# A second product whose two column groups are both 64 columns wide, in a recurrence with capacity-limited experts behind it

## The chip, the cores and the metric

The kernel runs on one core of one Trainium2 chip. The metric is the device time of one execution in microseconds (us). All inputs start in device memory (HBM) and the output ends there.

## The reference

Two blocks follow each other. The first is a gated recurrence over 4 sequences of 5,056 steps with 256 channels. The second takes its 20,224 rows as tokens, chooses one of 8 experts for each, keeps the 80 tokens of each expert with the highest gate, and gives only these an output; all other rows are zero.

```python
for t in range(S):
    h = f[:, t] * h + i[:, t] * x[:, t]
    y[:, t] = h
...
for e in range(E):
    ...
        keep = np.argpartition(-gw, capacity)[:capacity]
        tok_idx = tok_idx[keep]
    h = np.maximum(x[tok_idx] @ w1[e], 0.0)
    out[tok_idx] = gate_w[tok_idx, None] * (h @ w2[e])
```

`w1[e]` is 256 x 1024, `w2[e]` is 1024 x 256, both float32, so each is 1 MB. `h @ w2[e]` is the second product.

## The kernel before

The work goes through three stretches. In the first (to about 115 us) f and x are streamed in, turned with TensorE, scanned on VectorE and kept on chip as `h_all`; the router's logits are made on the way. In the second the 80 best tokens of each expert are ranked (lines 377 to 700) and their column numbers land in `trow`. In the third, the function `experts` (line 708), the tokens are collected, sent through the two products and scattered to the output. The change lies in the third alone.

`experts` runs over the 8 experts, e = 0 to 7. `gather(e)` (lines 717 to 728) copies 80 single columns of `h_all` into a tile `xe`; three engines share them, 24 on DVE, 32 on ACT and 24 on POOL, and each loads its column numbers from `trow` into registers first (line 723). `scaled(e)` (line 731, POOL) multiplies `xe`. `hidden(e)` (line 747, PE) is the first product: 32 matmuls, two for each of 2 x 8 pairs of a half of `w1` and a chunk of 128 hidden units. The two matmuls of a pair load 64 stationary columns each and write PSUM partitions 0 to 63 and 64 to 127, which are two column groups of the array; 80 columns move through. `relu(e)` brings the hidden values into the tile `hid`, the first half on ACT (line 754) and the second on DVE (line 755). `result(e)` (line 763, PE) is the second product: 8 chunks `c`, and for each chunk two matmuls with the hidden values of 64 and of 16 tokens as stationary columns, through which the 256 columns of a chunk of `w2` move into `y_ps`. `finish(e)` (line 771, DVE) multiplies by the gate into a row tile, and `scatter(e)` (line 775, POOL) is an indirect DMA of 80 rows to the output.

The order of the work is written out by hand in lines 799 to 839; nothing reorders it. Before the loop stand `gather` and `scaled` for experts 0, 1 and 2, `hidden(0)`, and two groups of idle matmuls (`busy`, line 160). Then, for each e: `relu(e)`, `hidden(e+1)`, `gather(e+3)`, `scaled(e+3)`, `result(e)`, `finish(e)`. So PE runs hidden(1), result(0), hidden(2), result(1), ..., hidden(7), result(6), result(7). Scatters 0 and 1 are issued around `gather(7)`; scatters 2 to 7 come after the loop, and five of them are held back until a named matmul of `result` has run (`apart`, line 814). Scatter 7 waits until all others have landed. Scatter 0 waits until the output has been cleared.

The weights come as 32 halves of 512 KB on SP's queue, which also carries the copies that clear the output (`copied`, line 137). The halves go round in 7 slots (`half`, lines 509 to 520), so half k is issued when PE has used half k - 7. The halves stand in the order in which PE uses them; the copies stand between them at fixed places (`BETWEEN`).

Each float32 matmul shows as two records in the trace; the word record means this below.

Of the kernel before, what the change touches and what calls it, by code (L numbers as in the profile page):

```python
# [9 lines left out]
F32 = mybir.dt.float32  # L10
# [5 lines left out]
ACT = mybir.ActivationFunctionType  # L16
PSUM = bass.MemoryType.PSUM
P = 128
# [8 lines left out]
def kernel(  # L27
# [11 lines left out]
    nc = tc.nc  # L39
    B, S, D = x.shape  # L40
    E, _, F = w1.shape
    N = B * S
    DC = D // P
    FC = F // P
    R = 4
# [4 lines left out]
    K = (capacity + TOP - 1) // TOP * TOP  # L50
# [20 lines left out]
    FH, CH = F // 2, FC // 2  # L71
# [13 lines left out]
    def slot(i, name):  # L85
        return ring[i].tile([P, R * D], F32, name=name, tag="buf")
# [36 lines left out]
    gates = consts.tile([K, E], F32, name="gates")  # L123
# [7 lines left out]
    def copied():  # L131

        at = written[0]
        n = min(P * ZH, TOTAL - at)
        if n:
            z = 2 * ZH if n % (2 * ZH) == 0 else D
            nc.sync.dma_start(out=out_flat[ds(at, n)].rearrange("(p k) -> p k", k=z),
                              in_=out_flat[:n].rearrange("(p k) -> p k", k=z))
            written[0] += n
# [22 lines left out]
    with tc.tile_pool(name="gsm", bufs=1) as gsm:  # L162
# [239 lines left out]
        with tc.tile_pool(name="plg", bufs=1, space=PSUM) as plg, \  # L402
# [48 lines left out]
            with tc.tile_pool(name="pct", bufs=4, space=PSUM) as pct:  # L451
                cts = {}

                def turn(*runs):
                    ct = pct.tile([P, 4 * P], F32, name="ct", tag="ct")
                    for g0, g1 in runs:
                        turned(ct[:, ds((g0 - runs[0][0]) * P, (g1 - g0) * P)], g0, g1)
                        cts[g0] = ct, runs[0][0]
                    return ct
# [24 lines left out]
                c = turn((6, LAST - 1), (LAST - 1, LAST))  # L484
# [222 lines left out]

    def experts(again):
        with tc.tile_pool(name="xp", bufs=3) as xp, \
             tc.tile_pool(name="mp", bufs=2) as mp, \  # L710
             tc.tile_pool(name="rp", bufs=E - R) as rp, \
             tc.tile_pool(name="psh", bufs=4, space=PSUM) as psh, \
             tc.tile_pool(name="psy", bufs=2, space=PSUM) as psy:
            w = {} if again else w_sb
            late = list(halves_of if again else halves_of[NSLOT - 1:])
            X, HID, Y, rows = {}, {}, {}, {}
            sent, marks = [], {}

            def gather(e):
                X[e] = xp.tile([P, DC, K], F32, name="xe", tag="xe")  # L720
                k = 0
                for engine, copy, n in ways:
                    _, at_tok = nc.values_load_multi_w_load_instructions(
                        trow[ds(e, 1), ds(k, n)], engines=(engine,), min_val=0, max_val=N - 1,
                        skip_runtime_bounds_check_because="column numbers come from iota")
                    for j, v in enumerate(at_tok):
                        copy(X[e][:, :, ds(k + j, 1)], h_all[:, :, ds(v, 1)])  # L727
                    k += n

            def scaled(e):  # L730
                nc.gpsimd.tensor_tensor(X[e], X[e], omlb.unsqueeze(2).broadcast_to([P, DC, K]),  # L731
                                        ALU.mult)

            H = P // 2

            def hidden(e):
                HID[e] = mp.tile([P, FC, K], F32, name="hid", tag="hid")
                xt = X.pop(e)
                wo = [w.pop((1, e, o)) for o in range(DC)]
                ps = [psh.tile([P, CH, K], F32, name="h_ps", tag="h_ps") for _ in range(2)]  # L740
                for o in range(DC):
                    for k in range(2 * CH):
                        i, c = divmod(k, CH)
                        a, j = divmod(c, J)
                        for s in range(2):
                            at = i * FH + a * J * P + j + J * s * H
                            nc.tensor.matmul(  # L747
                                ps[i][ds(s * H, H), c], wo[o][:, at:at + J * (H - 1) + 1:J],
                                xt[:, o], start=o == 0 and c == 0, stop=o == DC - 1,
                                skip_group_check=True)  # L750
                return ps

            def relu(e, ps):
                nc.scalar.activation(HID[e][:, :CH], ps[0], ACT.Relu)  # L754
                nc.vector.tensor_scalar_max(HID[e][:, CH:], ps[1], 0.0)

            def result(e):
                halves = [w.pop((2, e, i)) for i in range(2)]
                hid = HID.pop(e)
                y = Y[e] = psy.tile([K, D], F32, name="y_ps", tag="y_ps")  # L760
                for c in range(FC):
                    for s0, n in ((0, H), (H, K - H)):
                        marks[e, c] = nc.tensor.matmul(  # L763
                            y[ds(s0, n)], hid[:, c, ds(s0, n)], halves[c // CH][:, c % CH],
                            start=c == 0, stop=c == FC - 1, skip_group_check=True)

            def finish(e):
                if e == 0:
                    rows["y"] = slot(0, "y").rearrange("p (t d) -> p t d", t=R)
                rows[e] = rows["y"][:K, e] if e < R else rp.tile([K, D], F32, name="y4", tag="y4")  # L770
                nc.vector.tensor_scalar_mul(rows[e], Y.pop(e), gates[:, ds(e, 1)])  # L771

            def scatter(e, behind=None):

                sent.append(nc.gpsimd.indirect_dma_start(  # L775
                    out=out, out_offset=bass.IndirectOffsetOnAxis(ap=goal[:, ds(e, 1)], axis=0),
                    in_=rows.pop(e), in_offset=None, bounds_check=N - 1, oob_is_err=False))
                if behind:
                    tc.add_manual_dep(sent[-1].ins, marks[behind].ins.name, mybir.DependencyInfo(
                        mybir.DependencyClass.Sync, mybir.DependencyReason.DATA), reason="apart")  # L780
                for other in sent[:-1]:
                    if e < E - 1:
                        tc.declare_no_dep(sent[-1].ins, other.ins, reason="other rows")
                    else:
                        tc.add_manual_dep(sent[-1].ins, other.ins.name, mybir.DependencyInfo(
                            mybir.DependencyClass.Sync, mybir.DependencyReason.DATA),
                            reason="all rows")

            def more(m):
                for _ in range(2 * m):  # L790
                    if late:
                        k = len(halves_of) - len(late)
                        key = late.pop(0)
                        w[key] = half(*key)
                        if not again:
                            for _ in range(BETWEEN.count(k)):
                                copied()

            if again:
                more(3)  # L800
            gather(0)
            scaled(0)
            if not again:
                busy(psy, 4, "y_ps")
            gather(1)
            scaled(1)
            gather(2)
            scaled(2)
            ps = hidden(0)
            more(1)  # L810
            if not again:
                busy(psy, 3, "y_ps")

            apart = {2: (E - 3, FC - 1), 3: (E - 2, 0), 4: (E - 2, FC - 1), 5: (E - 1, 1),
                     6: (E - 1, FC - 2)}
            for e in range(E):
                relu(e, ps)
                if e == 0 and not again:
                    gates_of(slots[:, 1])
                if e + 1 < E:  # L820
                    ps = hidden(e + 1)
                    more(1)
                if e == E - 4:
                    scatter(0)
                if e + 3 < E:
                    gather(e + 3)
                    scaled(e + 3)
                if e == E - 4:
                    scatter(1)
                result(e)  # L830
                more(1)
                finish(e)
                if e == 0 and not again:
                    found = consts.tile([1, 1], F32, name="found")
                    nc.vector.tensor_reduce(found, total, AX.X, ALU.add)
                    nc.vector.tensor_copy(doubt, found)
                    rows_of(consts, slots[:, 0], slots[:, 1])
            for e in range(2, E):
                scatter(e, apart.get(e))
# [6 lines left out]
    with tc.If(unsure > 0):  # L846
        with tc.tile_pool(name="all", bufs=1) as sel, \
# [37 lines left out]
            rp = psa.tile([E, K], F32, name="rp")  # L885
# [46 lines left out]
```

## Time and profile before

| | us |
|---|---|
| median of 3 runs (252.64 to 252.92) | 252.69 |
| the profiled execution, its own time | 253.41 |
| its span in the trace | 251.5 |

| engine | busy us | share of the span |
|---|---|---|
| PE | 221.4 | 88% |
| DVE | 156.8 | 62% |
| ACT | 133.1 | 53% |
| POOL | 143.2 | 57% |

The busy shares are averages over three stretches that have different limits. For this change the third stretch, from about 142 us to the end, is the one to read: in order of time, and engine by engine. The span is 1.9 us shorter than the execution's own time; the rest lies around the traced instructions.

### The profile page before, as it was taken

To read this page: it belongs to the slowest core of one execution; us is meant where nothing else is said; L and a number is where in the kernel's file an instruction comes from. 1 tells how busy PE (TensorE), PEld (TensorE's weight loads), DVE (VectorE), ACT (ScalarE), POOL (GpSimd) and SP (SyncE) were. 2 spreads that over 40 slices of the span, in tenths; PEclk is the share of its full clock that TensorE was granted. 3 is DMA by queue.
4 is the path that set the end of the run, shared out by engine and by line. 5 is a ranking of instruction groups with operands and counts; after the bars stand their busy time and mean duration, and the time that the engine had idled before them with its cause. 6 is when DMAs were issued, how large, how long until landed. Compare 5 with 4: busy or idle time off the path is not lost.

```text
span 251.5 us, 6853 instructions
## 1 busy us (share of the span) xinstructions
PE 221.4 (88%) x2223; PEld 141.9 (56%) x2223; DVE 156.8 (62%) x400; ACT 133.1 (53%) x419; POOL 143.2 (57%) x287
## 2 busy tenths in 40 slices
PE   0699899899989998999966899799999999999960
PEld 0698787778868787777834646252525344352210
DVE  4189699999999999899999567435415051010100
ACT  4488798779787886888826066755042300000000
POOL 4678797889788798779844067650450620011211
PEclk9999999999999999999997979999999999999996
DMA  6999999999999999999999999969985474620000
GB/s 248 377 410 449 371 425 412 418 420 401 412 405 408 397 434 391 395 403 412 400 363 417 416 444 402 417 257 345 340 300 199 154 250 137 219 95 14 26 20 17
DMA packets 21363, 80.61 MB, mean 320 GB/s; under 512 B 2580, under 2 KB 2710, under 8 KB 20888
## 3 DMA queue, kind: packets, MB, share of 16 engines
q1 hardware_dynamic: 20936, 79.45, 80.4%
q0 software_dynamic: 384, 0.66, 0.9%
q8 instruction: 19, 0.31, 0.5%
q14 instruction: 24, 0.20, 0.2%
HBM read 72.62 MB, written 21.36 MB: 374 GB/s over the span
## 4 chain that ended last, share of the span: by engine, by line
PE 45%; issue 19%; ACT 10%; DVE 9%; DMA 9%; POOL 4%; ACTq 1%; DVEq 0%; POOLq 0%; SPq 0%
PE y_ps L763 14%; PE sp L251 11%; PE up L259 9%; PE lg L289 6%; DMA x_t<-in_x_dram 5%; ACT h_all L268 4%; ACT xe L727 3%; PE h_ps L747 3%; DMA f_t<-in_f_logit_dram 3%; DVE h_all L276 3%; POOL out_dram L775 2%; PE lt L313 2%; POOL x_t L245 2%; ACT ls L298 2%; DMA out_dram<-y,goal 1%
## 5 line engine op out<-in xcount | busy, mean ns | idle before, releaser
L245 POOL TENSOR_TENSOR x_t<-f_t,x_t 128x1024 f32<-128x1024 f32 x40 | 94.7, 2370 | 21.1 <-DMA x_t<-in_x_dram 10.6
L276 DVE TENSOR_TENSOR_SCAN h_all<-h_all,up 128x512 f32<-128x512 f32 (+1 forms) x80 | 95.8, 1244 | 9.9 <-PE up L259 6.4
L763 PE MATMUL y_ps<-w_sb,hid 128*64 128x256 f32 (+1 forms) x256 | 71.3, 393 | 1.4 <-ACT hid L754 1.4
L268 ACT ACTIVATE h_all<-sp,nomlb 128x512 f32<-128x512 f32 (+1 forms) x80 | 50.3, 677 | 16.5 <-PE sp L251 15.7
L763 PEld LDWEIGHTS y_ps<-w_sb,hid 128*64 128x64 f32 (+1 forms) x256 | 19.4, 115 | 50.4 <-issue 48.8
L241 ACT ACTIVATE f_t<-f_t 128x1024 f32<-128x1024 f32 x40 | 42.3, 1058 | 9.8 <-DMA f_t<-in_f_logit_dram 7.3
L259 PE MATMUL up<-ident,x_t 128*128 128x128 f32 x320 | 44.0, 278 | 2.8 <-DVE h_all L276 2.2
L251 PE MATMUL sp<-ident,f_t 128*128 128x128 f32 x320 | 45.4, 287 | 0.0
L251 PEld LDWEIGHTS sp<-ident,f_t 128*128 128x128 f32 x320 | 35.9, 145 | 7.8 <-issue 7.1
L259 PEld LDWEIGHTS up<-ident,x_t 128*128 128x128 f32 x320 | 36.7, 143 | 5.1 <-DVE h_all L276 3.7
L771 DVE TENSOR_SCALAR y<-y_ps,gates 80x256 f32<-80x256 f32 x8 | 3.8, 480 | 57.0 <-PE y_ps L763 51.5
L727 ACT COPY xe<-h_all 128x2 f32 x256 | 25.4, 190 | 18.8 <-issue 12.2
L727 POOL COPY xe<-h_all 128x2 f32 x192 | 24.3, 189 | 14.2 <-issue 7.0
L727 DVE COPY xe<-h_all 128x2 f32 x192 | 22.7, 173 | 12.0 <-issue 7.4
L775 POOL DMA_INDIRECT out_dram<-y,goal x8 | 7.5, 942 | 35.3 <-PE y_ps L763 31.1
L289 PE MATMUL lg<-h_all,wg 128*32 128x128 f32 (+1 forms) x640 | 26.4, 282 | 0.6 <-ACT ls L298 0.6
L754 ACT ACTIVATE hid<-h_ps 128x320 f32<-128x320 f32 x8 | 3.5, 435 | 39.2 <-PE h_ps L747 21.3
L747 PEld LDWEIGHTS h_ps<-xe,w_sb 128*64 128x64 f32 x512 | 18.2, 138 | 4.1 <-issue 3.6
L747 PE MATMUL h_ps<-xe,w_sb 128*64 128x80 f32 x512 | 19.5, 234 | 0.0
L289 PEld LDWEIGHTS lg<-h_all,wg 128*32 128x32 f32 x640 | 15.4, 108 | 7.0 <-issue 4.9
L731 POOL TENSOR_TENSOR xe<-xe,omlb 128x160 f32<-128x160 f32 x8 | 3.6, 452 | 23.5 <-DVE xe L727 22.1
L160 PE MATMUL warm<-h_all,ident 128*128 128x512 f32 x22 | 13.1, 740 | 0.0
(128 smaller groups left out, 105.6 us busy)
## 6 DMA issues: line engine op xcount, KB each, us to landing
f_t<-in_f_logit_dram SPq DMA_DIRECT2D x40, 512.0 KB, 6.6
x_t<-in_x_dram SPq DMA_DIRECT2D x40, 512.0 KB, 6.9
w_sb<-in_moe_w_dram SPq DMA_DIRECT2D x31, 512.0 KB, 5.0
out_dram<-out_dram SPq DMA_DIRECT2D x26, 512.0 KB, 8.2
out_dram<-zbuf SPq DMA_DIRECT2D x12, 512.0 KB, 10.0
out_dram<-h_all SPq DMA_DIRECT2D x1, 512.0 KB, 8.2
w_sb<-in_moe_w_dram SPq DMA_DIRECT2D x2, 256.0 KB, 2.8
out_dram<-out_dram SPq DMA_DIRECT2D x1, 256.0 KB
```

Of the source, the lines that this page charges most:

```text
L160: nc.tensor.matmul(warm, ident, h_all[:, 0, :4 * P], start=True, stop=True)
L241: nc.scalar.activation(s_t, s_t, ACT.Sigmoid, scale=-1.0)
L245: nc.gpsimd.tensor_tensor(u_t, sts[n], u_t, ALU.mult)
L251: nc.tensor.transpose(ps[:, ds(r * P, P)], sts[n][:, r, ds(o * P, P)], ident)
L259: nc.tensor.transpose(ps[:, r::R], uts[n][:, r, ds(o * P, P)], ident)
L268: nc.scalar.activation(columns(n, o).rearrange("p (k r) -> p k r", r=R), sps.pop((n, o)).rearrange("p (r k) -> p k r", r=R)[:, P - run(n / ...
L276: nc.vector.tensor_tensor_scan(h, h, ups.pop((n, o)), h_all[:, o, ds(spot(n - B) + G - 1, 1)] if n >= B else 0.0, ALU.mult, ALU.add)
L289: nc.tensor.matmul(lgs[g][ds(q * LC, LC), b, :k].rearrange("p (m i) -> p m i", i=2), wg[:, o], pairs[:, :, q], start=o == 0, stop=o == DC ...
L727: copy(X[e][:, :, ds(k + j, 1)], h_all[:, :, ds(v, 1)])
L747: nc.tensor.matmul(ps[i][ds(s * H, H), c], wo[o][:, at:at + J * (H - 1) + 1:J], xt[:, o], start=o == 0 and c == 0, stop=o == DC - 1, skip_ ...
L763: marks[e, c] = nc.tensor.matmul(y[ds(s0, n)], hid[:, c, ds(s0, n)], halves[c // CH][:, c % CH], start=c == 0, stop=c == FC - 1, skip_grou ...
L775: sent.append(nc.gpsimd.indirect_dma_start(out=out, out_offset=bass.IndirectOffsetOnAxis(ap=goal[:, ds(e, 1)], axis=0), in_=rows.pop(e), i ...
```

## The change

The second product's stationary operand is now always 64 columns wide. For the second group these are the remaining 16 tokens of chunk `c` and the 48 values that follow them in memory, which are the first hidden values of the next chunk. The results of these 48 columns land in PSUM partitions 80 to 127 of `y_ps`, which `finish` does not read. For the last chunk the 48 values lie behind the tile's end, so the tile is made 48 columns longer and these columns are set to zero once. For that, the two `hid` tiles are allocated once instead of anew for each expert, and the row tiles for experts 4 to 7 go from 4 buffers to 3.

```diff
-             tc.tile_pool(name="mp", bufs=2) as mp, \
-             tc.tile_pool(name="rp", bufs=E - R) as rp, \
+             tc.tile_pool(name="mp", bufs=1) as mp, \
+             tc.tile_pool(name="rp", bufs=E - R - 1) as rp, \
...
-                HID[e] = mp.tile([P, FC, K], F32, name="hid", tag="hid")
+                HID[e] = both[e % 2]
...
-                nc.scalar.activation(HID[e][:, :CH], ps[0], ACT.Relu)
-                nc.vector.tensor_scalar_max(HID[e][:, CH:], ps[1], 0.0)
+                hid = HID[e][:, :FC * K].rearrange("p (c k) -> p c k", k=K)
+                nc.scalar.activation(hid[:, :CH], ps[0], ACT.Relu)
+                nc.vector.tensor_scalar_max(hid[:, CH:], ps[1], 0.0)
...
-                y = Y[e] = psy.tile([K, D], F32, name="y_ps", tag="y_ps")
+                y = Y[e] = psy.tile([P, D], F32, name="y_ps", tag="y_ps")
+
                 for c in range(FC):
-                    for s0, n in ((0, H), (H, K - H)):
+                    for s in range(2):
                         marks[e, c] = nc.tensor.matmul(
-                            y[ds(s0, n)], hid[:, c, ds(s0, n)], halves[c // CH][:, c % CH],
+                            y[ds(s * H, H)], hid[:, ds(c * K + s * H, H)],
+                            halves[c // CH][:, c % CH],
                             start=c == 0, stop=c == FC - 1, skip_group_check=True)
...
-                nc.vector.tensor_scalar_mul(rows[e], Y.pop(e), gates[:, ds(e, 1)])
+                nc.vector.tensor_scalar_mul(rows[e], Y.pop(e)[:K], gates[:, ds(e, 1)])
...
+            both = [mp.tile([P, FC * K + P - K], F32, name=f"hid{i}") for i in range(2)]
+            for hid in both:
+                nc.gpsimd.memset(hid[:, FC * K:], 0.0)
             gather(0)
```

On PE the place is `result(0)` and what stands around it; a row names the output, the inputs, and the output's partitions x columns. Before:

```order
L747 MATMUL h_ps<-xe,w_sb 64x80 x32
L763 MATMUL y_ps<-w_sb,hid 64x256
L763 MATMUL y_ps<-w_sb,hid 16x256
L763 MATMUL y_ps<-w_sb,hid 64x256
L763 MATMUL y_ps<-w_sb,hid 16x256
```

And with the change:

```order
L747 MATMUL h_ps<-xe,w_sb 64x80 x32
L765 MATMUL y_ps<-w_sb,hid_4843 64x256 x16
L747 MATMUL h_ps<-xe,w_sb 64x80 x32
L765 MATMUL y_ps<-w_sb,hid_4844 64x256 x16
L747 MATMUL h_ps<-xe,w_sb 64x80 x32
```

The number of matmuls and their order stay; the alternation of 64 and 16 output partitions becomes a run of 16 alike.

On POOL the place is the head of `gather(0)`, after the last of the ranking's products (`what`, line 644); the names in brackets are the engines whose semaphores a row waits for:

```order
 L644 TENSOR_TENSOR what<-terms,mine 128x96 [waits Pool_49]
+L806 MEMSET hid_2117 128x48 [waits PE_49,DVE_49,Activation_49,Pool_49]
+L806 MEMSET hid_2118 128x48
 L723 TENSOR_LOAD trow [waits DVE_49]
 L727 ISA
-L727 COPY xe<-h_all 128x2 [waits PE_49,DVE_49,Activation_49,Pool_49]
+L727 COPY xe<-h_all 128x2
```

The wait for PE, which stood at the first copy, now stands at the first memset, ahead of the register loads of line 723. It is a wait for the same matmul as before, the last of line 684.

## Rows read from the trace of the kernel before

**Rows 1.** The page: the chain that ended last, by line; and the granted PE clock in 40 slices.
```profile
PE y_ps L763 14%; PE sp L251 11%; PE up L259 9%; PE lg L289 6%; DMA x_t<-in_x_dram 5%; ACT h_all L268 4%; ACT xe L727 3%; PE h_ps L747 3%; DMA f_t<-in_f_logit_dram 3%; DVE h_all L276 3%; POOL out_dram L775 2%; PE lt L313 2%; POOL x_t L245 2%; ACT ls L298 2%; DMA out_dram<-y,goal 1%
...
PEclk9999999999999999999997979999999999999996
```

**Rows 2.** The chain in order of time, from 158 us: start us, us, what.
```profile
158.49 8.96 PE y_ps L763 x32
167.46 2.37 PE h_ps L747 x64
169.82 8.74 PE y_ps L763 x32
```

**Rows 3.** Line 763 on PE: duration ns min/median/max, first and last start us, forms.
```profile
L763 PEld LDWEIGHTS y_ps<-w_sb,hid x256: 92/114/137, 158.5 to 242.4; 128*64 128x64 f32 x64, 128*16 128x16 f32 x64
L763 PE MATMUL y_ps<-w_sb,hid x256: 379/379/430, 158.5 to 242.6; 128*64 128x256 f32 x64, 128*16 128x256 f32 x64
```

**Rows 4.** Weight loads in order of time: the idle matmuls, then the head of result(0).
```profile
153.25 0.19 PEld L160 LDWEIGHTS warm<-h_all,ident 128*128 128x128 f32 x1 [0.24 <-issue]
153.68 0.19 PEld L160 LDWEIGHTS warm<-h_all,ident 128*128 128x128 f32 x1 [0.24 <-issue]
...
159.07 0.11 PEld L763 LDWEIGHTS y_ps<-w_sb,hid 128*16 128x16 f32 x2 [0.39 <-issue]
159.60 0.19 PEld L763 LDWEIGHTS y_ps<-w_sb,hid 128*64 128x64 f32 x2 [0.42 <-issue]
```

**Rows 5.** Stretches: us, busy of five engines, granted PE clock, DMA share, GB/s.
```profile
152.00:158.50 6.50, 5.07 (x71) 3.20 (x71) 3.57 (x28) 4.44 (x43) 4.77 (x35) 1.00 1.03 418
200.70:211.80 11.10, 11.10 (x97) 4.63 (x96) 3.68 (x26) 0.44 (x1) 1.39 (x2) 1.00 0.60 198
```

**Rows 6.** Timeline of ACT, POOL and DVE in the first experts' rounds, 158 to 180 us.
```profile
160.03 3.34 ACT L727 COPY xe<-h_all 128x2 f32 x32 [1.59 <-issue]
...
159.94 3.06 POOL L727 COPY xe<-h_all 128x2 f32 x24 [1.24 <-issue]
...
171.83 2.81 DVE L727 COPY xe<-h_all 128x2 f32 x24 [1.23 <-issue]
...
179.00 0.48 DVE L755 TENSOR_SCALAR hid<-h_ps 128x320 f32<-128x320 f32 x1
```

**Rows 7.** DMA issues, KB, us to landing: 157.45 to 158.0 us; then 162.9 to 189.9 us.
```profile
out_dram<-out_dram SPq DMA_DIRECT2D x1, 512.0 KB, 10.2
...
w_sb<-in_moe_w_dram SPq DMA_DIRECT2D x10, 512.0 KB, 4.9
out_dram<-out_dram SPq DMA_DIRECT2D x4, 512.0 KB, 5.4
out_dram<-out_dram SPq DMA_DIRECT2D x1, 256.0 KB
```

**Rows 8.** The experts' start: timeline and chain, 142 to 159 us; POOL's line 731 (page).
```profile
144.52 3.05 POOL L727 COPY xe<-h_all 128x2 f32 x24 [5.96 <-PE slots L684]
...
142.37 2.16 ACTq L723
...
144.16 5.40 PE L160 MATMUL warm<-h_all,ident 128*128 128x512 f32 x8
...
151.85 2.84 PE L160 MATMUL warm<-h_all,ident 128*128 128x512 f32 x6
...
158.01 0.43 ACT L754 ACTIVATE hid<-h_ps 128x320 f32<-128x320 f32 x1
...
L731 POOL TENSOR_TENSOR xe<-xe,omlb 128x160 f32<-128x160 f32 x8 | 3.6, 452 | 23.5 <-DVE xe L727 22.1
```

**Rows 9.** The end of the chain: start us, us, what.
```profile
242.18 3.13 DMA out_dram<-y,goal
...
246.21 0.83 POOL out_dram L775
```

## The prediction

> **What bounds the kernel now.** I read the chain that ended last first, then the same chain in order of time, then the order of PE's weight loads inside one second product, and only then the other engines and the DMA queue, since they decide how much of a gain on PE is kept.
>
> The chain gives 14% of the span to the second product, line 763, more than to any other line, and 3% to the first, line 747 [rows 1]. In order of time it is unbroken from 158.49 us on: one second product of 8.96 us, one first product of 2.37, the next second product of 8.74 [rows 2]. The last record of line 763 starts at 242.6 us and lasts 0.38, so PE ends at 243.0 [rows 3]. PE's stretch is then 243.0 - 158.49 = 84.5 us. It holds eight second products and six first ones, hidden(2) to hidden(7): 84.5 - 6 x 2.37 = 70.3, which is 8.79 us for each second product.
>
> Why a second product takes 8.8 us is seen in its pieces. It has 8 chunks, so 1.1 us per chunk of two matmuls, four records. [...]
>
> [...]
>
> **The change part by part.**
>
> *The pair of 64 and 64.* Its cost has no row of its own, so I bound it by the nearest. Below: two groups quite side by side, 32 records x 0.215 / 2 = 3.44 us. Above: the first product's 37 ns per record of 80 columns, overhead and all, stretched to 256 columns: 32 x 37 x 256/80 = 3.79 us. I take 3.5, near the lower end, since what 37 ns has over 33.5 looks like a fixed cost per record. If nothing else limits, PE's stretch becomes 8 x 3.5 + 6 x 2.37 = 42.2 us and ends at 158.49 + 42.2 = 200.7, which is 42.3 us sooner.
>
> *The other engines.* A round of PE falls from 11.2 us to 3.5 + 2.37 = 5.87. In a round ACT loads registers and copies, 1.59 + 3.34 us [rows 6], and does one relu, 0.43 [rows 8]: 5.36. DVE has 1.23 + 2.81 for its copies and 0.48 for the relu, as much again for `finish` [rows 6]: 5.0. POOL has 1.24 + 3.06 [rows 6] and 0.45 for line 731 [rows 8]: 4.75. All fit under 5.87, so I count them at nothing; with a second product under 3.0 us ACT would be late next.
>
> *The weights.* This is what I expect to be late next. At 157.50 a copy is issued that lands 10.2 us later, at 167.7 [rows 7]: eight transfers stand in the queue, and from then on they land in the order of issue. Behind it, up to the first half that result(4) needs, stand 10 halves and 4.5 copies [rows 7], 14.5 pieces of 512 KB. Now PE's slow pace spreads them over 32 us. With the change their slots come free early enough to keep the queue filled, so they land one after another. The price of a piece: 418 GB/s in the full queue [rows 5] is 1.25 us; in the stretch of weights alone 198 GB/s at a share of 0.60 [rows 5] is 330 GB/s if it were full, 1.59 us. I take 1.32, near the full queue's row because here too it never runs empty. Then the half lands at 167.7 + 14.5 x 1.32 = 186.8. PE alone would want it after result(0) to (3) and hidden(2) to (5), at 158.49 + 4 x 3.5 + 4 x 2.37 = 182.0. So PE waits 4.9 us by then, in several pieces. The 11 halves behind it land by 186.8 + 14.5 = 201.3, before PE needs the last. After result(4) starts, four second and two first products remain, 18.7 us: PE ends at 205.6 instead of 243.0, **-37.4 us**.
>
> *The memsets.* POOL now waits for the ranking's last product ahead of its register loads, which used to run during that wait: the copies began at 144.52, as soon as that product was done [rows 8]. So the loads, 1.24 us by POOL's later rows [rows 6] and at most ACT's 2.16, and two memsets of 48 columns, each under the 0.45 us of line 731 [rows 8], come on top: 1.3 to 3.0 us later, I take 1.8. Behind them on POOL stand gather(0) to (2) and the scalings that hidden(0) to (2) wait for. It is covered: hidden(0) stood behind idle matmuls until 149.56 and hidden(1) until 154.69, and result(0) waits for ACT's relu, which ends at 158.44 because ACT first does gather(2) [rows 8]; ACT isn't held up. hidden(1) would have to come 1.4 us late or more before result(0) felt it. Cost 0; without that cover up to 1.8.
>
> *Memory.* One row tile fewer makes finish(7) wait until scatter 4 has landed. Scatter 4 is let go at the end of result(6), about 202.3, issues and lands within some 3.1 us like the longest shown [rows 9]: 205.4, against result(7)'s end at 205.6. Cost 0, by little. Scatter 0 waits for the last clearing copy, which now lands at about 185, and gather(7) stands behind it on POOL; some 6 us later, by 191, it is ready, and hidden(7) wants it at about 196. Cost 0.
>
> *The tail.* Scatter 6 is let go by chunk 6 of result(7), its landing takes 3.13 us, and only then does scatter 7 go [rows 9]. Chunk 6 ended 1.1 us before PE's end and will end 0.44 before it; the tail hangs on the chunk, so it reaches 0.7 us further beyond PE's end: **+0.7**.
>
> Sum: -37.4 + 0.7 = -36.7. The profiled execution took 253.41 us, so 216.7 for one like it; it stands 0.72 above the median of 252.69, so I predict **216.0 us**.
>
> **The rivals.**
>
> 1. *The weights never hold PE up* (12%). For it: in the experts' later stretch the queue is busy for 0.60 only. Then the end is 200.7: 252.69 - 42.3 + 0.7 = 211.1.
> 2. *The clock falls when PE waits for weights* (10%). The granted clock did fall in two slices of this kernel [rows 1], around PE's waits in the ranking; the idle matmuls right after took 5.40 us for 8 records there and 2.84 for 6 later [rows 8]. If two second products ran at the lower level, 3.5 us more each: 223.
> [...]
> 4. *Every weight load is paid* (2%). If a load could not pass under the other group's matmul, each record would cost its load of 0.137 us [rows 3] besides its 0.107: 7.8 us, 8 us less in all, 245. The first product speaks against it too: its 64 records take 37 ns each, less than one load.
>    [...]
> 5. *Slower: the groups are as separate as now, and the wider load is on the path* (3%). From the 64 wide to the 16 wide load it is 0.58 us (158.49 to 159.07), back 0.53 [rows 2, 4]: the wide load's 0.05 is paid today. If separation has nothing to do with the widths, 64 matmuls pay 0.05 more: +3.2, 255.9. It decides if a chunk still takes over 1.12 us.
>
> **How the numbers follow.** The forecast has 69%. Its own ends: transfers at 1.25 us, -1.0; at 1.59, +3.9; a second product of 3.79, +1.2 behind the wait. The range reaches from rival 1, 211, to rival 2, 223, which also takes in the forecast's upper end, 221.1. What lies above has 9%, and a little below 211. A measurement here tells 0.2%, half a microsecond, from no change. Faster: all but rival 5, 0.96 with something kept back; slower 0.03; same 0.01.
>
> **What would show it.** In the changed profile a chunk of line 765 should take about 0.44 us, and a second product that doesn't wait 3.4 to 3.8. PE's idle time should name weights' landings, from result(2) or (3) to about result(4), some 5 us in sum, and little after. The DMA share should stay near 1 to about 185 us. POOL's first copy should begin near 146.3, with result(0) still near 158.5. I am wrong in the main point if records of line 765 follow each other by 0.2 us; wrong in the second if PE's idle time names ACT, DVE or POOL instead of DMA.

## The result, and the profile after

The changed kernel takes 215.81 us (median of 4 runs, 215.46 to 217.44), the kernel before 252.81 beside it (252.64 to 253.36). The ratio is 0.8546, with a 95% interval from 0.8501 to 0.8591. The prediction was 216.0, in a range from 211 to 223. The profiled execution took 215.72 us, with a span of 213.9.

The lines of the second product: the page's row before, then, after, the page's row and the line on its own, which answers to [rows 3]. In the page's rows the numbers behind the bar are busy us, mean ns, and idle us before with what ended it:

```profile
L763 PE MATMUL y_ps<-w_sb,hid 128*64 128x256 f32 (+1 forms) x256 | 71.3, 393 | 1.4 <-ACT hid L754 1.4
...
L765 PE MATMUL y_ps<-w_sb,hid 128*64 128x256 f32 x256 | 30.2, 381 | 2.9 <-ACT hid L755 2.0
...
L765 PE MATMUL y_ps<-w_sb,hid x256: 379/379/431, 158.5 to 204.4; 128*64 128x256 f32 x128
```

The count and the duration of a record have hardly moved: 256 records, 379 ns in the median, before and after. A record's own duration, 0.38 us, is longer than the 0.215 us by which the records of one group follow one another (158.97, 159.18, 159.40 us in the changed kernel, where the other group's begin at 158.97, 159.19, 159.41), and doesn't tell whether two share the time. What tells is when the line starts and stops: the last record began at 242.6 and begins at 204.4. The busy time of the line, in which simultaneous records count once, went from 71.3 us to 30.2.

PE in order of time, after (start us, us, what, idle time before and its releaser); the rows answer to [rows 2]:

```profile
158.48 3.67 PE L765 MATMUL y_ps<-w_sb,hid 128*64 128x256 f32 x32 [0.43 <-ACT hid L755]
161.99 2.38 PE L747 MATMUL h_ps<-xe,w_sb 128*64 128x80 f32 x64
...
172.61 1.95 PE L765 MATMUL y_ps<-w_sb,hid 128*64 128x256 f32 x16 [0.36 <-DMA w_sb<-in_moe_w_dram]
175.32 2.51 PE L747 MATMUL h_ps<-xe,w_sb 128*64 128x80 f32 x64 [0.77 <-DMA w_sb<-in_moe_w_dram]
179.41 1.95 PE L765 MATMUL y_ps<-w_sb,hid 128*64 128x256 f32 x16 [1.57 <-ACT hid L755]
181.92 1.95 PE L765 MATMUL y_ps<-w_sb,hid 128*64 128x256 f32 x16 [0.56 <-DMA w_sb<-in_moe_w_dram]
...
186.36 3.67 PE L765 MATMUL y_ps<-w_sb,hid 128*64 128x256 f32 x32
189.83 2.41 PE L747 MATMUL h_ps<-xe,w_sb 128*64 128x80 f32 x64
192.05 3.65 PE L765 MATMUL y_ps<-w_sb,hid 128*64 128x256 f32 x32
...
197.71 7.11 PE L765 MATMUL y_ps<-w_sb,hid 128*64 128x256 f32 x64
```

Two things are to be seen. A second product that doesn't wait takes 3.5 us from its start to the next line's (158.48 to 161.99), where it took 8.9. And from 172 to 186 us PE waits again and again, mostly for halves of the weights. The wait of 1.57 us is put down to ACT, but that relu belongs to the next expert; the half that result(3) needs was issued at 168.64 and took 10.6 us, so it landed at 179.28, just before that product began. PE ends at 197.71 + 7.11 = 204.82 instead of 243.0. Its stretch from 158.5 went from 84.5 us to 46.3, 38.2 less; the tail behind it went from 8.5 us to 9.1. Together that is 37.6 us, the whole change of the span.

Stretches, after: us, busy of PE, weight loads, DVE, ACT and POOL, granted PE clock, DMA share, GB/s; they answer to [rows 5]:

```profile
170.30:179.40 9.10, 6.41 (x101) 4.48 (x96) 6.84 (x51) 7.02 (x66) 6.31 (x47) 1.00 0.99 397
...
192.00:197.70 5.70, 5.70 (x104) 5.01 (x101) 0.88 (x2) 0.47 (x2) 0.91 (x1) 1.00 1.02 395
197.70:204.90 7.20, 7.12 (x71) 5.42 (x66) 0.92 (x3) 0.19 (x1) 2.97 (x4) 1.00 0.30 103
```

The DMA queue, 0.60 busy in the later experts before [rows 5], is now full until nearly all weights have landed, with a share of 0.99 to 1.06 in each stretch from 158.5 to 197.7 us. The engines' busy shares alone would hide this: PE is still the busiest of them, at 84%. The granted clock stayed at 1.00 through PE's waits.

POOL's head and the end of the chain, after, which answer to [rows 8, 9]:

```profile
144.80 0.21 POOL L806 MEMSET hid<- 128x48 f32 x2 [6.68 <-PE slots L684]
146.82 3.00 POOL L727 COPY xe<-h_all 128x2 f32 x24 [1.82 <-issue]
...
204.67 3.17 DMA out_dram<-y,goal
...
208.74 0.83 POOL out_dram L778
```

The memsets wait as foreseen, POOL's copies begin at 146.82 instead of 144.52, and result(0) begins at 158.48 instead of 158.49. The late start is covered.

### The profile page after: what moved, and what is told of

It reads as the page before. It is cut to its first block, busy times and chain, and to the rows that moved or that the text cites. A ratio compares the mean times of both kernels' runs of the same rounds, so it can differ in the third digit from the quotient of the medians.

```text
span 213.9 us, 6843 instructions
## 1 busy us (share of the span) xinstructions
PE 178.7 (84%) x2223; PEld 142.2 (66%) x2223; DVE 157.4 (74%) x400; ACT 132.7 (62%) x419; POOL 143.7 (67%) x289
## 4 chain that ended last, share of the span: by engine, by line
PE 42%; DMA 22%; ACT 10%; DVE 9%; issue 9%; POOL 4%; POOLq 1%; SPq 1%; DVEq 0%; ACTq 0%
PE sp L251 13%; PE up L259 10%; DMA out_dram<-out_dram 9%; PE lg L289 8%; DMA f_t<-in_f_logit_dram 6%; ACT h_all L268 5%; PE warm L160 4%; DVE h_all L276 3%; PE lt L313 3%; DMA w_sb<-in_moe_w_dram 3%; DMA h_all<-in_moe_w_gate_dram 3%; POOL out_dram L778 2%; PE h_ps L747 2%; ACT ls L298 2%; PE slots L684 2%
## 5 line engine op out<-in xcount | busy, mean ns | idle before, releaser
L251 PE MATMUL sp<-ident,f_t 128*128 128x128 f32 x320 | 44.5, 283 | 0.0
L251 PEld LDWEIGHTS sp<-ident,f_t 128*128 128x128 f32 x320 | 35.1, 142 | 7.7 <-issue 7.3
L765 PE MATMUL y_ps<-w_sb,hid 128*64 128x256 f32 x256 | 30.2, 381 | 2.9 <-ACT hid L755 2.0
L765 PEld LDWEIGHTS y_ps<-w_sb,hid 128*64 128x64 f32 x256 | 20.0, 137 | 10.7 <-ACT hid L755 2.3
L747 PEld LDWEIGHTS h_ps<-xe,w_sb 128*64 128x64 f32 x512 | 19.3, 138 | 3.5 <-POOL xe L731 1.5
L747 PE MATMUL h_ps<-xe,w_sb 128*64 128x80 f32 x512 | 20.0, 234 | 0.8 <-DMA w_sb<-in_moe_w_dram 0.8
L160 PE MATMUL warm<-h_all,ident 128*128 128x512 f32 x22 | 12.5, 711 | 0.0
L313 PE MATMUL lt<-ident,ls 128*128 128x128 f32 (+1 forms) x40 | 7.4, 308 | 5.1 <-ACT ls L298 5.1
```

Source lines behind the costliest of these rows:

```text
L160: nc.tensor.matmul(warm, ident, h_all[:, 0, :4 * P], start=True, stop=True)
L251: nc.tensor.transpose(ps[:, ds(r * P, P)], sts[n][:, r, ds(o * P, P)], ident)
L313: nc.tensor.transpose(lts[g0][:k, g - g0, j], ls[:, j::R], ident)
L747: nc.tensor.matmul(ps[i][ds(s * H, H), c], wo[o][:, at:at + J * (H - 1) + 1:J], xt[:, o], start=o == 0 and c == 0, stop=o == DC - 1, skip_ ...
L765: marks[e, c] = nc.tensor.matmul(y[ds(s * H, H)], hid[:, ds(c * K + s * H, H)], halves[c // CH][:, c % CH], start=c == 0, stop=c == FC - 1 ...
```

## The experiments

My theory had three parts: mixed widths keep the two groups apart and pay for each change; equal widths run them side by side; and what is then left on the table is PE waiting for weights behind the clearing copies. Each run below attacks one of them. On the chips of these runs the kernel before took 252.4 to 256.2 us, more spread than at first; in the ranking, ahead of PE's stretch, the last products of line 684 took 2.5 us in some executions and 4.2 in others. The difference goes with the granted clock: over these products it was 1.00 in the kernel before, where they took 2.46 us, and 0.66 in the changed kernel, where they took 3.39. The ranking lies ahead of the change and isn't touched by it. So single executions are compared by PE's own stretch, from the start of result(0), more than by the whole time.

### One matmul for all 80 tokens

Against the kernel before:

```diff
-                    for s0, n in ((0, H), (H, K - H)):
-                        marks[e, c] = nc.tensor.matmul(
-                            y[ds(s0, n)], hid[:, c, ds(s0, n)], halves[c // CH][:, c % CH],
+                    marks[e, c] = nc.tensor.matmul(
+                        y, hid[:, c], halves[c // CH][:, c % CH],
```

> The second product with one matmul per chunk, all 80 tokens as one stationary operand, in the memory layout of the kernel before. My theory: what counts is how often the 256 columns pass one after another; a mixed pair passes them twice plus two changes, an equal pair or a single group once. 16 records x 0.215 = 3.44 us and two changes between 64 and 80 wide per expert, some 0.24: 3.7 us per second product, 215.5 to 218 us in all. Rival (a weight load is hidden only under the other group's matmul): each record also pays its load, 16 x (0.215 + 0.137) = 5.6 us, 8 x 2.1 = 17 us more on PE of which the wait for weights, some 5 us, absorbs a part: 225 to 231 us.

It took 216.35 us, ratio 0.8487 (0.8428 to 0.8546), not to be told from the changed kernel. PE in order of time:

```profile
158.13 3.68 PE L762 MATMUL y_ps<-w_sb,hid 128*80 128x256 f32 x16 [0.15 <-ACT hid L754]
161.75 2.44 PE L747 MATMUL h_ps<-xe,w_sb 128*64 128x80 f32 x64
...
192.17 3.68 PE L762 MATMUL y_ps<-w_sb,hid 128*80 128x256 f32 x16
195.78 2.44 PE L747 MATMUL h_ps<-xe,w_sb 128*64 128x80 f32 x64
198.15 7.13 PE L762 MATMUL y_ps<-w_sb,hid 128*80 128x256 f32 x32
```

Half the records, and at 3.6 us nearly the same time as the pair's 3.5. So the price of a second product is how often its 256 columns pass through the array one after another: once per chunk for one group of 80, once for two groups side by side, twice for a mixed pair. The rival, that weight loads come to lie open with one group, falls. A round without waits is 198.15 - 192.17 = 5.98 us here and 197.71 - 192.05 = 5.66 in the changed kernel; both kernels also wait for weights, at the same places.

### Widths 64 and 32, and 64 and 48

Against the changed kernel, with 48 in place of 32 for the second run:

```diff
-                    for s in range(2):
+                    for s0, n in ((0, H), (H, 32)):
                         marks[e, c] = nc.tensor.matmul(
-                            y[ds(s * H, H)], hid[:, ds(c * K + s * H, H)],
+                            y[ds(s0, n)], hid[:, ds(c * K + s0, n)],
```

> As the changed kernel, but the second group takes 32 stationary columns instead of 64 (16 tokens and 16 unread). [...] Rival (only a group of 16, which fills no column group of the array, is slow): chunks of 0.44 us, 215 to 217 us.

> As the changed kernel, but the second group takes 48 stationary columns, 16 tokens and 32 unread. [...] Rival (only exactly equal widths run side by side): chunks of 1.1 us, 252 to 257.

My forecast was 251 to 254 us with 32, as slow as the kernel before, and 214.5 to 217 with 48, as quick as 64 and 64. With 32 it took 256.12 us in a single execution, beside 255.07 for the kernel before; with 48, 217.16 us, ratio 0.8518 (0.8447 to 0.8588). The head of PE's stretch, with 32 first, then with 48:

```profile
159.74 9.07 PE L765 MATMUL y_ps<-w_sb,hid 128*64 128x256 f32 x32 [1.34 <-ACT hid L755]
168.74 2.44 PE L747 MATMUL h_ps<-xe,w_sb 128*64 128x80 f32 x64
```

```profile
157.81 3.67 PE L765 MATMUL y_ps<-w_sb,hid 128*64 128x256 f32 x32 [0.96 <-ACT hid L755]
...
180.50 1.93 PE L765 MATMUL y_ps<-w_sb,hid 128*64 128x256 f32 x16 [1.57 <-DMA w_sb<-in_moe_w_dram]
```

With 32 a second product is 9.0 us, as with 16; with 48 it is 3.5. So the widths needn't be equal, and 16 is not slow for being narrow: beside a group of 64, 48 goes as quickly as 64, while 32 and 16 don't. Where between 32 and 48 that turns, and by what mechanism, no run shows. In this trace the wait of 1.57 us that was put down to ACT in the changed kernel is put down to the weights.

### The loops swapped, one group after the other

The same edit on both kernels, here on the one before; on the changed one `for s in range(2)` goes outside in the same way:

```diff
-                for c in range(FC):
-                    for s0, n in ((0, H), (H, K - H)):
+                for s0, n in ((0, H), (H, K - H)):
+                    for c in range(FC):
```

> The kernel before with the two loops of the second product swapped: first all 8 chunks with 64 columns, then all 8 with 16. Theory: one change instead of sixteen, and the groups still one after another: 32 x 0.215 = 6.9 us and a change, 7.0 instead of 8.8, 8 x 1.8 = 14 us less: 237 to 240 us. Rival (the 16 wide matmul itself is slow, alternating or not): no difference, 252 to 254 us.

> The changed kernel with the two loops swapped: first all 8 chunks of the first group, then all 8 of the second. [...] Rival (equal widths alone make it, whatever the order): 215 to 217 us.

With 64 and 16 it took 243.2 us, with 64 and 64, 229.92, each in a single execution. PE in order of time, with 64 and 16:

```profile
143.13 4.16 PE L684 MATMUL slots<-what,put 128*80 128x8 bf16 x60
...
161.19 7.22 PE L763 MATMUL y_ps<-w_sb,hid 128*64 128x256 f32 x32 [0.86 <-ACT hid L754]
168.34 2.44 PE L747 MATMUL h_ps<-xe,w_sb 128*64 128x80 f32 x64
```

A second product takes 7.1 us, as forecast (7.0), against 8.9 before: 32 records one after another and one change. The whole is 3.2 us above the upper end of the expectation; 2.7 of them are that PE's stretch begins late, at 161.19 instead of 158.49, behind a ranking in which line 684 took 4.16 us. So the changes between groups, some 1.8 us per second product or 0.12 for each of the fifteen fewer, and the separation of the groups, some 3.6, are two prices, and the change takes both away.

With 64 and 64 my expectation missed: I had put it at 237 to 240 us, with the 32 records of the two groups one after another, 6.9 us. PE, and then the records of `y_ps` in four equal stretches of the first second product (us, busy of PE with the records that run in the stretch, of weight loads and of DVE, clock, DMA share, GB/s):

```profile
158.36 5.67 PE L765 MATMUL y_ps<-w_sb,hid 128*64 128x256 f32 x29 [1.05 <-ACT hid L755]
163.65 0.36 PE L747 MATMUL h_ps<-xe,w_sb 128*64 128x80 f32 x2
```

```profile
158.36:159.66 1.30, 1.30 (x6) 0.88 (x7) 0.00 (x0) 1.00 1.15 477
159.66:160.96 1.30, 1.30 (x7) 0.82 (x6) 0.00 (x0) 1.00 0.71 293
160.96:162.26 1.30, 1.30 (x11) 0.98 (x10) 0.00 (x0) 1.00 0.90 359
162.26:163.56 1.30, 1.30 (x8) 0.83 (x7) 0.00 (x0) 1.00 1.23 490
```

A count takes in records that began before the stretch and still run. It is 7 or 8 where one record begins every 0.215 us, 6 in the first stretch, before which none began, and 11 in the third, where the loop goes from the first group to the second. Taken one by one, the records there form two trains of even spacing: the first group's last four begin at 161.00, 161.22, 161.43 and 161.65 us, the second group's first four at 161.01, 161.27, 161.49 and 161.70. So the second group begins when the first has three records yet to begin, and four of each run side by side: the two needn't be neighbours in the program, but no more than these four overlap. The same is seen at the seam to the next first product, whose records begin at 163.65 between those of line 765. A round takes 8.1 us (166.73 to 174.83; 229.92 in all), which lies between my forecast and the rival's: the order matters, by 2.4 us a round against the changed kernel, but less than I had put it.

### Three groups of 32

Against the changed kernel:

```diff
-                    for s in range(2):
+                    for s in range(3):
                         marks[e, c] = nc.tensor.matmul(
-                            y[ds(s * H, H)], hid[:, ds(c * K + s * H, H)],
+                            y[ds(s * 32, 32)], hid[:, ds(c * K + s * 32, 32)],
```

> Three groups of 32 stationary columns per chunk, 80 tokens and 16 unread, 24 matmuls for each second product. Theory (any number of groups of one width run side by side): chunks of 0.44 to 0.5 us and two changes of width per round, 215 to 219. Rival (only two groups at a time): 48 records x 0.215 / 2 = 5.2 us, 1.7 more than two groups of 64; 8 x 1.7 = 13.6 less some 5 of waits, 223 to 226.

218.91 us in a single execution. PE:

```profile
159.82 3.65 PE L765 MATMUL y_ps<-w_sb,hid 128*32 128x256 f32 x48 [0.47 <-ACT hid L755]
163.41 2.44 PE L747 MATMUL h_ps<-xe,w_sb 128*64 128x80 f32 x64
```

48 records in the time of 32: three groups run side by side as well as two. The stretch began 1.3 us later than in the changed kernel, which is a little under half of what the whole time lies above it; the rest is the stretch itself, 48.0 us against 46.3, with rounds of 5.95 us like those of the single group of 80.

### The memory part alone

The changed kernel with `for s0, n in ((0, H), (H, K - H))` in place of the equal groups, so with the longer `hid` tiles, the memsets and the three row buffers.

> The changed kernel's memory, memsets and buffers with the matmuls of before, 64 and 16 columns. Theory (memsets and buffers are covered and the whole gain is the matmuls'): within 0.5 us of the kernel before on the same chip. Rival (a part of the gain or a loss is theirs, such as POOL's later start): 1 to 2 us off.

254.09 us against 254.0, ratio 1.0023 (0.9985 to 1.0062): the kernel before. POOL's head and PE's start:

```profile
144.26 0.21 POOL L806 MEMSET hid<- 128x48 f32 x2 [5.75 <-PE slots L684]
146.28 3.03 POOL L727 COPY xe<-h_all 128x2 f32 x24 [1.82 <-issue]
```

```profile
158.47 8.96 PE L765 MATMUL y_ps<-w_sb,hid 128*64 128x256 f32 x32 [0.99 <-ACT hid L755]
```

POOL's copies begin 1.8 us later than in the kernel before, and result(0) at 158.47 all the same. The whole gain is the matmuls'.

### Without the late copies

In `more`, in the changed kernel, and in a second run in the one with a single group of 80:

```diff
                             for _ in range(BETWEEN.count(k)):
-                                copied()
+                                if k < 12:
+                                    copied()
+                                else:
+                                    written[0] += min(P * ZH, TOTAL - written[0])
```

> The changed kernel without the last 4.5 pieces of clearing copies, those that stand between the weights from half 12 on; it leaves out the clearing of their rows. Theory (PE's waits from result(2) to result(4) come from the copies that stand ahead of the weights): the waits go. Six rounds of 5.69 us and the last two products, 7.1, from 158.5 on end at 199.7 instead of 204.8, 5.1 us less: 210.2 to 211.5. Rival (the gathers on ACT, POOL and DVE would hold PE at the same places): 214.5 to 216.

> One matmul per chunk with all 80 tokens, without the last 4.5 pieces of clearing copies (their rows' clearing is left out). Theory: with the waits gone PE's own rounds show, 5.98 us here against 5.69 for the pair, since there are two changes of width per round and no overlap of the first product with the second: 6 x 0.29 more than the run with the pair and no copies, 1.7 us, 212 to 213. Rival (the two forms cost PE the same): equal to that run.

211.15 us, ratio 0.8319 (0.8273 to 0.8364), with the pair; 213.71, ratio 0.8404 (0.8356 to 0.8451), with one group. PE in order of time with the pair, and its stretches as above:

```profile
187.45 3.62 PE L765 MATMUL y_ps<-w_sb,hid 128*64 128x256 f32 x31
...
193.14 7.07 PE L765 MATMUL y_ps<-w_sb,hid 128*64 128x256 f32 x63
```

```profile
170.30:179.40 9.10, 9.10 (x136) 6.83 (x134) 6.93 (x52) 7.01 (x66) 6.29 (x46) 1.00 1.03 393
```

PE has no gap from 170.3 to 179.4 us, where it was idle for 2.7 us before the copies were taken out. It ends at 200.2, 41.7 us after result(0) began, against 46.3: the copies cost PE 4.7 us. ACT, POOL and DVE do the same work in this run and hold nothing up, so the rival falls. The single group is 2.6 us behind the pair here, where 1.7 was expected. By PE's own stretch it is 1.9 us, 43.5 against 41.7, of which 0.26 is one wait for weights; the stretch also began 0.6 us later, which isn't the group's doing. So the expected 1.7 is borne out: with the weights out of the way, the 0.3 us that a round with equal widths is shorter does count.

### The copies later

In the changed kernel the last five copies are put further back, and scatters 0 and 1 behind the scaling of expert 7's tokens:

```diff
-    BETWEEN = (7, 8, 8, 10, 12, 13, 15, 16, 18)
+    BETWEEN = (7, 8, 8, 10, 17, 19, 21, 23, 25)
...
-                if e == E - 4:
-                    scatter(0)
                 if e + 3 < E:
                     gather(e + 3)
                     scaled(e + 3)
                 if e == E - 4:
+                    scatter(0)
                     scatter(1)
```

> The changed kernel with the last five copies put behind halves 17, 19, 21, 23 and 25 instead of 12, 13, 15, 16 and 18, and scatters 0 and 1 both after the scaling of expert 7's tokens, since they wait for the last copy. Theory: PE's waits shrink to under 1.5 us; but the DMA queue, full until 201.5 us, then limits the last product, so PE ends at about 202.4: 2 to 2.5 us less than the changed kernel, 213 to 214.5. Rival (the later copies delay the scatters, and the tail loses what PE gains): 215.5 to 217.

217.64 us, ratio 0.8539 (0.8498 to 0.8579): no gain over the changed kernel's 0.8546. PE in order of time, and stretches:

```profile
160.58 3.67 PE L765 MATMUL y_ps<-w_sb,hid 128*64 128x256 f32 x32 [0.45 <-ACT hid L755]
...
185.25 3.67 PE L765 MATMUL y_ps<-w_sb,hid 128*64 128x256 f32 x32 [1.27 <-DMA w_sb<-in_moe_w_dram]
...
192.67 3.67 PE L765 MATMUL y_ps<-w_sb,hid 128*64 128x256 f32 x32 [1.27 <-DMA w_sb<-in_moe_w_dram]
...
199.11 0.39 PE L747 MATMUL h_ps<-xe,w_sb 128*64 128x80 f32 x5 [0.36 <-issue]
...
200.23 7.07 PE L765 MATMUL y_ps<-w_sb,hid 128*64 128x256 f32 x63
```

```profile
185.00:200.00 15.00, 12.40 (x187) 10.21 (x189) 3.17 (x17) 2.14 (x17) 5.28 (x20) 1.00 1.02 405
```

The waits have moved from results 2 to 4 to results 4 and 5 and hidden(7), which is stretched from 2.4 us to about 4 by small gaps that name no releaser; why, was not tried. PE's stretch is 207.3 - 160.58 = 46.7 us, as long as in the changed kernel. The queue is full in both arrangements (a share of 1.02 from 185 to 200 us here), and what is put behind the weights at one place stands ahead of other weights at the next. That the full queue is the reason is argued from this and not shown by a run of its own. No run beat the changed kernel with the whole computation in it.

## Why the prediction was right

**What bounded the kernel.** The second product's two passes per chunk and the changes between them: shown, by the pieces. 64 and 16 alternating take 8.9 us, 64 and 16 in two runs 7.1, 64 and 64 3.5.

**The pair of 64 and 64.** 3.5 us was taken and 3.5 measured. The round is a little better than the sum, 5.66 to 5.70 us instead of 5.87, mainly because the first product, put at 2.37 us, takes 2.2 from its start to the next line's (189.83 to 192.05): between products of one width no change is paid. Where hidden(7) follows, a group's last record of line 765 begins at 195.32 us and its first of line 747 at 195.54, 0.22 later, as within a product; behind a single group of 80 that step is 0.31 (195.48 to 195.79). Of the numbers behind the 3.5, the 0.215 us per record is the step that the records show; the 33.5 ns and a fixed cost per record on top are shown by no run. Pairs of the first product's records begin 0.069 us apart in the kernel before (167.51 to 169.59), 35 ns per record, and the rest of the 37 lies at the product's ends, such as 0.12 us behind its first pair (167.39 to 167.51). That a change of group costs 0.12 us is shown by the run with 64 and 16 by group, and that the price goes with the widths by the runs with 32 and 48; why it does was not shown. Rivals 4 and 5 each needed a chunk of 0.98 us or more, where it is 0.44, and both fall.

Weight loads are not on the path in these two forms: with 64 and 64 a pair of records with their two loads of 137 ns takes 3.5 / 16 = 0.22 us, where the two loads alone would be 0.27; even with a single group of 80 columns a record and its load take 3.6 / 16 = 0.22 together.

**The other engines.** Counted at nothing, and right: without the copies PE had no gap in the stretch where ACT was busiest.

**The weights.** This was the term with the widest bounds. The half that result(4) needs was forecast for 186.8 us; it was issued at 176.53 and took 9.7 us, so it landed at 186.2, and result(4) began at 186.36, against 182.0 for PE alone. The waits were put at 4.9 us in all and are 4.7 by the run without the copies. The gaps in PE's rows sum to 3.3 only: a row ends with its last record, which lasts 0.38 us where the next can begin 0.215 behind its start, so a gap hides some 0.16 us, and the wait for result(4)'s half shows no gap at all. And the longest gap, 1.57 us, names ACT, which by the prediction's own sign would have spoken against it; the landing at 179.28 and the run with 64 and 48 show that it is the weights. The price of 1.32 us per piece was a choice between 1.25 and 1.59. It measured 1.31 (13.5 pieces from 168.6, when the half issued at 160.50 landed, to 186.2), because the queue stayed full, as assumed; that it came so near is in part luck. One sign was put too narrowly: the DMA share was to stay near 1 to about 185 us, and it stays at 1.02 up to 197.7. The sum itself went further and had the last half land by 201.3, and it landed at 201.5. PE then isn't late, but the queue has nothing to spare. The expectation for the run with later copies knew of the full queue; it failed because it let PE's waits shrink, and they moved.

**Memsets, buffers, tail.** POOL's copies were put 1.8 us further behind the ranking's last product; it is 2.0 (144.80 to 146.82), and covered. finish(7) ran at 204.86, right behind PE. The tail grew by 0.6 us, forecast 0.7.

**The sum.** It had 36.7 us, and the trace's span is 37.6 shorter: the half of result(4) landed 0.6 us earlier, and the rounds behind it are shorter by 0.3 in all. The medians differ by 37.0, so that 216.0 stands against 215.81 is nearer than the terms are, which is luck.

**Rival 1**, no wait for weights, didn't come, but its price is borne out: the kernel without the late copies takes 211.15 us against the 211.1 worked out for it. **Rival 2**, a falling clock, didn't come: the granted clock was 1.00 through the waits, none of which was over 1.6 us.

## What to carry to other kernels

Count a TensorE stage by how often the moving columns pass one after another, not by its matmuls: here two column groups passed together at 64 with 64 and at 64 with 48 (3.5 us for a second product), and a rest of 16 or 32 beside 64 cost its own pass and two changes per chunk (8.9 and 9.0). If all columns go into one group, as the 80 do here, a single matmul can do as well as the pair, within the noise here (216.35 and 215.81 us), and needs no padding. Before trusting a large gain on PE, lay the queue of transfers that feeds it against the new pace, piece by piece: here that took 4.7 us of 42 back, and the one rearrangement within the full queue that was tried didn't return it.

## What the runs showed of the hardware that was not expected

Beside a group of 64 stationary columns, one of 48 takes as long as one of 64 (3.5 us for the second product), one of 32 about as long as one of 16 (9.0 and 8.9). Two groups of 64 overlap without being neighbours in the program: with the loops swapped, the second group's first four records begin beside the last four of the first group's (161.01 to 161.70 and 161.00 to 161.65 us). Between the first and the second product of one width no change is paid (a step of 0.22 us, where it is 0.31 behind a group of 80), which makes a round 0.3 us shorter than with a single group of 80 (5.66 and 5.98). Scatter 0, issued into the full queue, took 5.2 us to land, and scatter 4, behind the last weights, 2.3 (us to landing, in the changed kernel):

```profile
out_dram<-y,goal POOLq DMA_INDIRECT x1, 5.2
...
out_dram<-y,goal POOLq DMA_INDIRECT x1, 2.3
```

The prediction had taken about 3.1 us for the landing on which finish(7) waits; had scatter 4, issued at 201.65, met the full queue and taken 5.2, it would by this estimate have landed at 206.9, and finish(7), which ran at 204.86, would have waited for it.
